# Reordering the loads of the second batch, and three edits to the chains of the first two batches, in a linear-attention and mixer kernel

## The chip, the cores and the metric

The kernel runs on one core of a Trainium2 chip. The metric is device time in microseconds (us). A ratio below is the mean time of one kernel's fast runs over the mean time of the fast runs of the kernel before in the same rounds on the same chip, so it is not quite the ratio of the medians quoted beside it (plain means of the listed runs give it within 0.001). Runs over 1.5% above the fastest of their kernel count as slow and are in no ratio. "Clock" is the mean granted TensorE clock of a run, 1 for full speed.

## The reference, cut to what matters

```python
# 8 batches, 8 heads, 576 positions, head width 64
q_p = phi(q); k_p = phi(k)            # relu times cos(pos), relu times sin(pos), side by side
kv  = einsum('bhsf,bhsd->bhfd', k_p, v)
z   = sum(k_p, axis=2)
x   = einsum('bhsf,bhfd->bhsd', q_p, kv) / (einsum('bhsf,bhf->bhs', q_p, z) + 1e-6)
u   = x + V^T U^T x                    # low-rank mixing over the positions
out = u + relu(u @ w_ch1) @ w_ch2      # w_ch1 is 512 x 2048, w_ch2 is 2048 x 512
```

The 576 positions are handled as four blocks of 128 (the "main" part) and a tail of 64. A main load of one batch is 1 MiB in 1 KB rows, a tail load 128 KB in 256 B rows.

## The kernel before: the parts concerned

TensorE runs a long stream of 512-wide matmuls: `g1` (u times w_ch1) and `g2` (hidden times w_ch2). Attention of a later batch is threaded into that stream. Only the first two batches have nothing to hide behind: `chain0` is batch 0's attention, `chain1` is batch 1's, woven into batch 0's `g1`. In the code, `V_`, `A_` and `G_` are VectorE, ScalarE and GpSimd.

```python
    V_four("X", 1)
    V_evac(V_)                                   # VectorE: V from PSUM to SBUF
    ...
    a0 = chain0()                                # GpSimd issues w1_load(0) just ahead, w1_load(1) in here
    alloc_q(1)
    load_main(qst[1], q, 1)                      # all of batch 1 on SyncE's queue
    load_tail(qt[1], q, 1)
    ...
    chain_end(0, a0)
    g1_main(0, 0, True)                          # first use of w1's first block
    ...
    def chain1(fill):
        kv_unit(1, 0, "T", 1)                    # heads 0-3: needs k features and v_ext
        fill(0)
        rec0 = den_unit(1, 0, 4, "X", 1)
        v_block(1, 4, 8, 0, 4, A_)
        ...                                      # kv_unit(1, 1) for heads 4-7 later
    ...
        at(2, lambda: v_prep(1, 0, H, (4,), (G_,)))     # GpSimd casts v's tail first ...
        at(2, lambda: v_block(1, 0, 4, 0, 4, G_))       # ... and then heads 0-3 of v's main part
```

GpSimd executes in order.

## Time and profile before

| | kernel before |
|---|---|
| time, first three runs | 319.07 us median (318.75 to 319.55) |
| span of the profile | 317.3 us |
| TensorE idle in the first 65 us / in the rest | 5.46 / 2.78 us |
| first `g1` matmul / first kv of batch 1 complete | 22.88 / 34.94 us |

The table is read from the front: TensorE is full once batch 1 is through, so a change to the front is worth what it moves the stream of `g1` matmuls, and no more. In the stretch from 22 to 36 us TensorE is busy for 11.92 of 14 us. The columns of such a line are the stretch, its length, then busy time and count of instructions of TensorE, its weight loads, VectorE, ScalarE and GpSimd, then clock, DMA share and GB/s:

```profile
22.00:36.00 14.00, 11.92 (x119) 7.11 (x119) 10.52 (x21) 11.10 (x18) 6.41 (x9) 1.00 1.18 250
```

### The profile page before, as it was taken

The numbers are of one execution on the slowest core, as the hardware profiler recorded it, in microseconds if no ns is written. First come the engines' busy times: TensorE is split into PE (matmuls) and PEld (weight loads), VectorE is DVE, ScalarE is ACT, GpSimd is POOL, SyncE is SP. The second block draws the span as 40 slices with busy tenths as digits, with TensorE's granted clock in tenths as the row PEclk, the third lists the DMA queues.
The fourth block names the chain that finished last, engine by engine and source line by source line (L and its number), as shares of the span: only waits on it lengthen the run. The fifth ranks groups of instructions, "written<-read, shape, count | busy, mean of one in ns | idle before, by whom it ended". The sixth has DMA issues, their size and how long they took to land.

```text
span 317.3 us, 5795 instructions
## 1 busy us (share of the span) xinstructions
PE 308.8 (97%) x2380; PEld 162.0 (51%) x2380; DVE 155.8 (49%) x355; ACT 151.5 (48%) x261; POOL 35.8 (11%) x67
## 2 busy tenths in 40 slices
PE   7979899999999999999999999999999999999996
PEld 3546554475545444474455444574454444464443
DVE  8769653843877554037826584254736510001211
ACT  5939655686806256659300187559300166650000
POOL 4405202100121220000121100000121100000000
PEclk9999999999999999999999999999999999999999
DMA  7999999954386928950999469900691130001122
GB/s 226 328 258 274 199 234 340 332 166 164 94 189 169 297 67 190 262 195 2 206 249 315 179 130 230 331 5 33 157 192 66 68 83 0 2 0 68 66 89 77
DMA packets 83803, 51.82 MB, mean 163 GB/s; under 512 B 52066, under 2 KB 81026, under 8 KB 83778
## 3 DMA queue, kind: packets, MB, share of 16 engines
q1 hardware_dynamic: 76850, 40.05, 46.7%
q0 software_dynamic: 6784, 11.35, 15.1%
q8 instruction: 18, 0.29, 0.4%
q10 hardware_dynamic: 144, 0.07, 0.1%
q14 instruction: 7, 0.06, 0.1%
HBM read 36.86 MB, written 9.44 MB: 146 GB/s over the span
## 4 chain that ended last, share of the span: by engine, by line
PE 87%; DMA 5%; ACT 4%; SPq 1%; DVE 1%; POOL 0%; issue 0%; DVEq 0%; ACTq 0%
PE o_ps L543 39%; PE g_ps L491 33%; PE gt_ps L511 4%; DMA w_bf<-in_moe_w_ch_dram 3%; PE kv_ps L262 3%; PE va_ps L407 3%; PE x_ps L363 3%; DMA vst<-in_v_dram 2%; ACT hid L500 2%; PE a_ps L390 1%; PE t_ps L279 1%; ACT k_p L228 1%; ACT q_p L228 1%; SPq L81 1%; SPq L75 0%; POOL mark L738 0%
## 5 line engine op out<-in xcount | busy, mean ns | idle before, releaser
L500 ACT ACTIVATE hid<-g_ps 128x512 bf16<-128x512 f32 x128 | 76.2, 596 | 100.8 <-PE g_ps L491 100.4
L491 PE MATMUL g_ps<-uT,w_bf 128*128 128x512 bf16 x512 | 118.5, 379 | 0.8 <-DMA w_bf<-in_moe_w_ch_dram 0.8
L543 PE MATMUL o_ps<-w_bf,hid 128*128 128x512 bf16 (+2 forms) x528 | 119.2, 373 | 0.0
L491 PEld LDWEIGHTS <-w_bf 128*128 128x128 bf16 x512 | 48.7, 98 | 56.8 <-DMA w_bf<-in_moe_w_ch_dram 1.0
L543 PEld LDWEIGHTS <-hid 128*128 128x128 bf16 x528 | 48.6, 98 | 52.8 <-issue 1.7
L553 DVE TENSOR_TENSOR o_sb<-u_bf,o_ps 128x512 f32<-128x512 bf16 (+2 forms) x33 | 22.1, 669 | 62.7 <-PE o_ps L543 62.7
L563 POOL DMA_DIRECT2D out_dram<-o_sb x24 | 13.4, 560 | 165.7 <-DVE o_sb L553 155.6
L408 DVE TENSOR_TENSOR u_bf<-x_bf,va_ps 128x512 bf16<-128x512 bf16 x32 | 21.8, 687 | 10.1 <-PE va_ps L407 10.1
L105 DVE CAST kv<-kv_ps 128x260 bf16<-128x260 f32 x14 | 6.0, 429 | 32.6 <-PE kv_ps L262 32.6
L373 DVE TENSOR_TENSOR x_bf<-x_ps,rec 128x512 bf16<-128x512 f32 x24 | 16.6, 691 | 0.8
L228 ACT ACTIVATE q_p<-qst,sinw 128x512 bf16<-128x512 f32 (+1 forms) x24 | 15.1, 658 | 2.2 <-DMA qst<-in_q_dram 2.1
L511 PE MATMUL gt_ps<-uT_tl,w_bf 128*128 128x128 bf16 x256 | 15.6, 219 | 0.0
L407 PE MATMUL va_ps<-A_sb,V_bf 128*128 128x512 bf16 x40 | 15.2, 379 | 0.0
L543 PE MATMUL o_ps<-w_bf,hid_tl 128*128 128x512 bf16 x64 | 15.1, 379 | 0.0
L313 DVE TENSOR_SCALAR rec<-x_ps 128x8 f32<-128x8 f32 (+1 forms) x30 | 5.0, 165 | 20.2 <-PE x_ps L363 20.1
L511 PEld LDWEIGHTS <-w_bf 128*128 128x128 bf16 x256 | 14.6, 98 | 0.5
L262 PEld LDWEIGHTS <-k_p 128*128 128x128 bf16 x256 | 11.5, 97 | 5.8 <-ACT k_p L228 1.2
L262 PE MATMUL kv_ps<-v_ext,k_p 128*128 128x65 bf16 x256 | 12.5, 193 | 1.6 <-ACT k_p L228 0.9
L230 DVE TENSOR_SCALAR k_p<-kst,cosw 128x512 bf16<-128x512 f32 (+1 forms) x31 | 14.0, 474 | 0.0
L518 ACT ACTIVATE hid_tl<-gt_ps 128x512 bf16<-128x512 f32 x16 | 9.4, 598 | 5.5 <-PE gt_ps L511 5.5
L363 PEld LDWEIGHTS <-q_pT 128*128 128x128 bf16 x192 | 9.1, 98 | 5.6 <-issue 0.6
L179 PE MATMUL w_ps<-zero 128*128 128x512 bf16 x35 | 10.7, 443 | 1.2 <-DVE U_bf L162 1.2
(106 smaller groups left out, 255.4 us busy)
## 6 DMA issues: line engine op xcount, KB each, us to landing
qst<-in_q_dram SPq DMA_DIRECT2D x7, 1024.0 KB, 8.7
kst<-in_k_dram SPq DMA_DIRECT2D x7, 1024.0 KB, 7.4
vst<-in_v_dram SPq DMA_DIRECT2D x6, 1024.0 KB, 8.3
out_dram<-o_sb POOLq DMA_DIRECT2D x24, 256.0 KB, 3.0
w_bf<-in_moe_w_ch_dram POOLq DMA_DIRECT2D x8, 512.0 KB, 9.9
vst<-in_v_dram SPq DMA_DIRECT2D x4, 512.0 KB, 7.6
out_dram<-o_sb SPq DMA_DIRECT2D x7, 256.0 KB, 2.3
qst<-in_q_dram SPq DMA_DIRECT2D x2, 512.0 KB, 3.7
```

The costliest lines, as they stand in the source:

```text
L228: nc.scalar.activation(out=o, in_=i, func=AF.Relu, bias=0.0, scale=w)
L230: eng.tensor_scalar(out=o, in0=i, scalar1=0.0, scalar2=w, op0=ALU.max, op1=ALU.mult)
L262: nc.tensor.matmul(out=acc[:, i, :], lhsT=k_p[b][:, c, h, :] if c < 4 else k_tl[:, h, :], rhs=vx[:, c, h, :], start=(c == 0), stop=(c == 4),)
L363: nc.tensor.matmul(out=acc[:, g, i * E : i * E + E], lhsT=qT_of(b, c, h), rhs=kv_sb[b][:, h, :], start=True, stop=True,)
L373: nc.vector.tensor_tensor(out=x_of(b, c, rows).rearrange("p (g i d) -> p g i d", g=2, d=D), in0=view[:, :, :, 0:D], in1=rec[rows].unsqueez ...
L407: nc.tensor.matmul(out=va, lhsT=V_bf[:, c, :], rhs=A_sb[b], start=True, stop=True)
L408: nc.vector.tensor_tensor(out=u_bf[b][:, c, :] if c < 4 else u_tl[b // 2][rows, :], in0=x_of(b, c, rows), in1=va[rows, :], op=ALU.add,)
L491: nc.tensor.matmul(out=g_ps.rearrange("p (c t) -> p c t", c=4), lhsT=w1_bf[:, d, j * P : j * P + P], rhs=uT[b][:, :, d, :], start=(d == 0) ...
L500: nc.scalar.activation(out=hid[b][:, j, :], in_=g_ps, func=AF.Relu, bias=0.0, scale=1.0)
L511: nc.tensor.matmul(out=g_ps[:, jj, :], lhsT=w1_bf[:, d, j * P : j * P + P], rhs=uT_tl[pr][:, d, :], start=(d == 0), stop=(d == 3),)
L543: nc.tensor.matmul(out=o[:, cols], lhsT=lhs[:, j, c * P : c * P + P], rhs=w2_bf[:, j, cols], start=(j == 0), stop=(j == NJ - 1),)
L553: nc.vector.tensor_tensor(out=o_sb[:, cols], in0=u[:, cols], in1=o[:, cols], op=ALU.add)
```

## The change

The intent: load what is needed first, first. Batch 1's main blocks and w1 go into one queue (GpSimd's, called the software queue, q0 in the profile) in order of use. The three tails stay on SyncE's hardware queue (q1), held back by a tiny DMA until batch 0's first reciprocals exist. Besides, V leaves PSUM behind v's cast, one x row goes to ScalarE, and batch 1's k features are made for heads 0-3 first, those of heads 4-7 behind the first kv.

```diff
     V_four("X", 1)
-    V_evac(V_)
...  in chain0
         v_block(0, 0, 4, 0, 3, V_)
+        V_evac(V_)
...
+        load_main(qst[1], q, 1, eng=G_)
         w1_load(1)
+        load_main(kst[1], k, 1, eng=G_)
+        load_main(vst[1], v, 1, 0, 4, G_)
+        load_main(vst[1], v, 1, 4, 8, G_)
+        w1_load(2)
+        nc.sync.dma_start(out=mark2, in_=rec0[0:1, 0, 0:1])
+        load_tail(qt[1], q, 1)
+        load_tail(kt[1], k, 1)
+        load_tail(vt[1], v, 1)
...
-            xh_unit(0, c, 4, 8, rec1, *(O2, O2, G3)[n])
+            xh_unit(0, c, 4, 8, rec1, *(O2, O2, G3)[n], A_ if n == 1 else None)
...  in chain1
+        for c in ORD[:3]:
+            k_prep(1, c, (V_, None), 4, 8)
         kv_unit(1, 0, "T", 1)
+        for c in ORD:
+            k_prep(1, c, (None, A_), 4, 8)
+        v_block(1, 4, 8, 0, 4, A_)
         fill(0)
         rec0 = den_unit(1, 0, 4, "X", 1)
-        v_block(1, 4, 8, 0, 4, A_)
+        for c in ORD[3:]:
+            k_prep(1, c, (V_, None), 4, 8)
...  in the main stream
-    alloc_q(1) ... all loads of batch 1 on SyncE's queue
-        at(..., lambda c=c, n=n: k_prep(1, c, (V_, A_)))
+        at(..., lambda c=c: k_prep(1, c, (V_, A_), 0, 4))
-    at(2, lambda: [w1_load(2), w1_load(3)])
+    at(6, lambda: w1_load(3))
```

More of the change, by code (lines that the diff above doesn't have):

```diff
@@ L672, in chain0 @@
         v_block(0, 4, 8, 2, 4, A_)
+        alloc_q(1)
+        alloc_k(1)
+        alloc_v(1)
+        load_main(qst[1], q, 1, eng=G_)
         w1_load(1)
+        load_main(kst[1], k, 1, eng=G_)
[6 more added lines that the diff above has]
+        load_tail(vt[1], v, 1)
         for n, c in enumerate(TL):
@@ L740 @@
     a0 = chain0()
-    alloc_q(1)
-    load_main(qst[1], q, 1)
-    load_tail(qt[1], q, 1)
-    alloc_k(1)
-    load_main(kst[1], k, 1)
-    load_tail(kt[1], k, 1)
-    alloc_v(1)
-    load_tail(vt[1], v, 1)
-    load_main(vst[1], v, 1, 0, 4)
-    load_main(vst[1], v, 1, 4, 8)
     chain_end(0, a0)
@@ L770 @@
         at(1 + n, lambda c=c, tg=tg: qtr_unit(1, c, eng=V_, tag=tg[0], bufs=tg[1]))
-        at((4, 5, 5, 6, 6)[n], lambda c=c, n=n: k_prep(1, c, (V_, A_)))
-    at(2, lambda: G_.tensor_copy(out=mark, in_=q_tlT[0:TS, 0, TS : TS + 1]))
-    at(2, lambda: [w1_load(2), w1_load(3)])
+        at((4, 5, 5, 6, 6)[n], lambda c=c: k_prep(1, c, (V_, A_), 0, 4))
     at(2, lambda: v_prep(1, 0, H, (4,), (G_,)))
     at(2, lambda: v_block(1, 0, 4, 0, 4, G_))
+    at(6, lambda: w1_load(3))
     at(6, lambda: [w2_load(n) for n in range(4)])
```

## The prediction

> **What bounds the kernel now.** I read the page first, then PE's waits, the table by stretches, the chain in order of time, the timeline of the first 50 us, and last the DMA queues in short stretches. From the page, the table by stretches, and the waits of PE in the first 130 us:
>
> ```profile
> PE 308.8 (97%) x2380; PEld 162.0 (51%) x2380; DVE 155.8 (49%) x355; ACT 151.5 (48%) x261; POOL 35.8 (11%) x67
> 0.00:65.00 65.00, 59.54 (x577) 33.36 (x578) 45.83 (x118) 43.28 (x82) 16.36 (x32) 1.00 1.09 269
> 65.00:317.00 252.00, 249.22 (x1807) 128.69 (x1804) 109.99 (x238) 108.27 (x180) 19.48 (x35) 1.00 0.50 136
> PE kv_ps L262 <- ACT k_p L228: 0.9, 2, 0.5
> PE g_ps L491 <- DMA w_bf<-in_moe_w_ch_dram: 0.8, 1, 0.8
> PE t_ps L279 <- DVE q_p L230: 0.7, 1, 0.7
> PE kv_ps L262 <- DVE v_ext L105: 0.5, 1, 0.5
> PE d_ps L321 <- ACT kv L103: 0.5, 1, 0.5
> ```
>
> TensorE is busy for 97% of the span. It is idle for 65.00 - 59.54 = 5.46 us in the first 65 us and for 2.78 us in the other 252. Everything the diff touches lies before 50 us, so its whole prize is inside those 5.46 us, of which 1.19 us pass before the first matmul. The matmuls themselves are the same in number and order in both kernels (I compared the two instruction streams of TensorE). This bounds the gain at about 4 us of 319, 1.3%.
>
> The first 65 us is also where the DMA is full: its mean share is 1.09 there against 0.50 afterwards. The waits that the change aims at, from the timeline:
>
> ```profile
> 9.61 0.82 DVE L105 CAST V_bf<-v_ps 128x640 bf16<-128x640 f32 x1 [0.69 <-PE v_ps L194]
> 12.58 0.55 DVE L105 CAST v_ext<-vst 128x768 bf16<-128x768 f32 x1
> ...
> 22.87 0.11 PEld L491 LDWEIGHTS <-w_bf 128*128 128x128 bf16 x2 [1.01 <-DMA w_bf<-in_moe_w_ch_dram]
> ...
> 33.64 0.10 PEld L262 LDWEIGHTS <-k_p 128*128 128x128 bf16 x1 [0.65 <-ACT k_p L228]
> ...
> 34.26 0.20 PE L262 MATMUL kv_ps<-v_ext,k_p 128*128 128x65 bf16 x1 [0.41 <-ACT k_p L228]
> ```
>
> A number in brackets is the idle time ahead of the row and who ended it. The first w1 block is issued by GpSimd at 13.12 and lands at 22.83: the chain of waits gives it 9.72 us. The queue table for 15 to 16, 16 to 17 and 17 to 25 us says why:
>
> ```profile
> q1 hardware_dynamic: 346, 0.35, 109.0%
> ...
> q0 software_dynamic: 6, 0.01, 3.6%
> ...
> q0 software_dynamic: 978, 0.98, 72.7%
> q1 hardware_dynamic: 1029, 0.93, 43.1%
> ```
>
> Columns are packets, MB written, share of 16 engines. Until 16.8 us only batch 1's q moves, on SyncE's queue; then w1 and batch 1's k alternate packet by packet, so each gets half the engines. The order is not the order of use.
>
> **What the Trainium skill says.** (1) "DMA: Bandwidth & Descriptors", Queues, rings and completion order: an engine round-robins between queue rows at packet granularity. The trace agrees: 978 against 1029 packets in 17 to 25 us. The same page, Issuing engines are not separate DMA queues: issuing from several engines adds no bandwidth. So one queue means order, not speed. (2) "SBUF — State Buffer", the box on the "DVE blocks DMA" trap: VectorE's two-port operations keep GpSimd from writing descriptors for its DMAs. The trace shows 3.7 us from issue to the first w1 packet, with VectorE busy for nearly all of 13.98 to 18.0, but also q1 full until 16.7; it does not say which of the two delays it. (3) "VectorE: DVE Perf Modes", The TRN2 errata: a fixed extra time per ScalarE or VectorE instruction. The trace agrees: on ScalarE a 128x512 k feature costs 0.72 us reported (about 0.61 from start to start), a 128x256 one 0.49 (about 0.43); a half costs more than half.
>
> **The change part by part.**
>
> *V evacuated later.* 0.82 us of VectorE leaves the front of v's cast. The cast starts at 12.58 now; the first v half landed at about 11.83, so it can start at 11.88, and VectorE's work ahead of it, moved up by 0.8, ends at about 11.85. It then ends at 12.43. The warm-up matmuls on TensorE end at 12.71, so the first kv starts there and not at 13.18: 0.47 us. The evacuation fits between 12.43 and 13.25, before the kv sums (13.47) want VectorE. Second v half and second k half land at 15.0 and 13.3, early enough, so the 0.47 travels on.
>
> *One x row to ScalarE.* In the second half of chain 0, VectorE loses one of five x multiplies (0.41 us) and ScalarE takes four 128x64 activations (0.93 us for the same set in the first half) where it sits idle for 0.98 us. VectorE's last x ends 0.41 + 0.47 us earlier. TensorE then goes on without the 0.2 to 0.4 us pauses around 21 us and reaches the first g1 matmul at about 21.4 instead of 22.88, if w1 is there: 1.4 us up to this point (0.84 of it the wait for w1).
>
> *Loads in one queue.* The order becomes w1(0), q, w1(1), k, v halves, w1(2), with the three tails on SyncE after the first reciprocals. Rates from the trace: q1 alone moves 0.36 MB/us; w1/w2 alone 0.205 MB/us written (3.09 MB in 30 to 46 us), so a 0.52 MB block takes 2.6 us; a 1.05 MB q or k takes 2.9; the tails (0.39 MB of small packets, 0.24 to 0.28 MB/us around 25.5 us) take 1.6 together. q1's bytes summed up to the end of v's second half of batch 0 reach that point at 13.7 us. After it, the changed kernel has only w1(0), whose first packets I put at 15.4 (2.3 us after issue; it was 3.7 and, for w1(2), 2.4). So the DMA idles for about 1.7 us where it was full. From there, with 1.3 us from last packet to landing: w1(0) 18.0, landing 19.3; q 20.9 plus the tails 22.5, landing 23.8; w1(1) landing 26.4; k 29.3; first v half 30.7; second 32.2; w1(2) 34.8.
>
> Against the needs: w1(0) at 21.4, met. q: its first main feature ran at 24.98, so -1.2 at best. w1(1) at about 26.8, met. k was used from 30.5, so -1.2. v half: GpSimd's cast of 1.04 us ends at 31.8; kv began at 32.89. w1(2): block 8 of g1 ran at 35.97 to 36.1; w1(2) at 34.8 lets it start 1.3 us earlier and no more.
>
> *k features by halves.* Ahead of kv(1,0) ScalarE has 5 half features, 5 x 0.43 = 2.2 us, instead of 3.4 (k_tl 0.72, k_p 1.33 and 1.32), and VectorE likewise. The two waits of 0.53 and 0.41 us inside kv go: 0.94 us. The later halves bring 2.2 us of ScalarE behind kv; it now idles 1.38 + 0.51 + 0.28 us between 35.65 and 39.0, so they fit without a wait for the second kv.
>
> *Sum.* 1.4 at g1's start plus 0.94 at kv would be 2.3 us, if the DMA did not matter. The landing of w1(2) caps it: all loads together are the same bytes over the same 16 engines, delivered about 1.7 us later in total because of the idle start. The cap gives 1.3 us. Behind 50 us nothing changes: TensorE is full and keeps the shift. So 319.07 - 1.3 = 317.8 us.
>
> **The rivals.** (a) *Transfers are not the limit*: w1(0) starts by 14.5 and the gain is the full 2.3 us: 316.7. For it: w1(0) began exactly when q's bulk packets ended, so the backlog of q1 may have held it, and that is gone. (b) *A new wait takes the place of the old one*: the software queue starts as late as before (16.8), or is slower with q's, k's and v's 1 KB pieces than q1 (no transfer of that kind is in this trace; w1's pieces are 1 KB written and 2 KB read, about 205 packets/us alone, against 350 on q1). Then q, v or w1(2) become the wait: first transposes of batch 1, kv(1,0) or g1's block 8, and the time is 319 to 320.5. For it: at 205 packets/us q takes 5 us instead of 2.9. Against it: the share of 118 to 125% of the engines at 205 packets/us says that those packets are just bigger jobs. (c) *ScalarE becomes the bound in chain 1* because of the later halves, two v_block and x work: a few tenths at most, since the slack above is 2.2 us; 318.2.
>
> **Range and chances.** Rival (a) sets the low end, a mix of the expected case with (b) the high end: 316.4 to 319.4. Both a gain and a loss of over 2% (6.4 us) are outside what 5.46 us of idle time, or one or two landings late by a few us, can do. Faster than 2%: 0.01; within: 0.97; slower: 0.02.
>
> **What would show each step.** V: the first kv without its 0.48 us wait for v_ext, starting at about 12.7. x and w1: first g1 matmul at 21.2 to 21.6, no wait for w_bf there. Queue: q0 from about 15.4 without a break to some 50 us, q1 nearly empty in 20 to 40; k landing at 29 to 30. Halves: no wait for k_p in kv(1,0); 128x256 ScalarE k features behind it. Cap: a wait of about 1 us for w_bf before g1's block 8, near 34.8. Wrong if TensorE waits at the transposes of q or at kv for over 1 us, if g1 starts after 22.5, or if the first 65 us have as much idle time as now.

## The result, and the profile after

The changed kernel took 323.84 us median of six runs (321.31 to 324.25), the kernel before 319.41 (318.75 to 324.39): ratio 1.0117, 95% interval 1.0069 to 1.0165. The ratio leaves out the slow run of 324.39; with it, it would be 1.009. It is slower by about 1%, where I had predicted 0.4% faster. The profiled execution ran 321.40 us with a span of 319.6 us. It is one of the two fastest of the six, so its trace accounts for 2.3 us of loss and not for the 4.4 us between the medians.

TensorE's waits in the first 130 us, to be held against those of the kernel before:

```profile
PE kv_ps L262 <- POOL v_ext L105: 2.1, 1, 2.1
PE w_ps L179 <- DVE U_bf L162: 1.2, 1, 1.2
PE t_ps L279 <- DVE q_p L230: 0.5, 1, 0.5
PE d_ps L321 <- ACT kv L103: 0.5, 1, 0.5
PE v_ps L189 <- DMA V<-in_moe_V_dram: 0.4, 1, 0.4
PE t_ps L279 <- ACT q_tl L228: 0.4, 1, 0.4
```

The two waits that the change aimed at are gone (w1 at the first `g1`, 0.8 us, and ScalarE's k features at kv, 0.9 us). In their place stands a wait of 2.1 us of kv for GpSimd. The timeline shows what GpSimd itself waited for, and what came behind it on TensorE:

```profile
21.66 0.59 PE L491 MATMUL g_ps<-uT,w_bf 128*128 128x512 bf16 x2
...
32.73 0.61 POOL L105 CAST v_ext<-vt 64x512 bf16<-64x512 f32 x1 [11.84 <-DMA vt<-in_v_dram]
33.40 1.04 POOL L105 CAST v_ext<-vst 128x1024 bf16<-128x1024 f32 x1
34.50 0.57 PE L262 MATMUL kv_ps<-v_ext,k_p 128*128 128x65 bf16 x4 [2.12 <-POOL v_ext L105]
...
36.60 1.87 PE L491 MATMUL g_ps<-uT,w_bf 128*128 128x512 bf16 x4
...
38.71 1.39 PE L491 MATMUL g_ps<-uT,w_bf 128*128 128x512 bf16 x4
```

Read it from the top. The first `g1` matmul runs at 21.66, 1.22 us earlier than before, and nothing waits for w1. Then GpSimd stands for 11.84 us on v's tail, a load of 128 KB. It was issued at 18.27 and landed 14.4 us later:

```profile
18.27 0.59 SPq L81 DMA_DIRECT2D vt<-in_v_dram  x1
```

The cast of v's main part has no wait of its own behind that: its data was there, and it stood behind the tail in GpSimd's order. By the packet records the last packet of the half of v that kv needs started at 29.3 us, the last one of v's tail at 32.2. No run changed the order of the two casts.

The queues between 22 and 32 us (packets, MB written, share of the 16 engines) show why a small load takes so long:

```profile
DMA packets 2461, 3.13 MB, mean 313 GB/s; under 512 B 1249, under 2 KB 1946, under 8 KB 2459
## 3 DMA queue, kind: packets, MB, share of 16 engines
q0 software_dynamic: 1275, 2.82, 94.3%
q1 hardware_dynamic: 1184, 0.29, 17.7%
```

Packets again alternate, 1275 against 1184. But SyncE's packets are rows of 256 B, one each, and the software queue's are 1 KB (w1) or 4 KB (q, k and v: four rows together). An equal share of turns gave SyncE's queue 0.29 of 3.13 MB. A tail has 64 x 8 = 512 rows, so 512 / 16 engines = 32 turns. The median duration of a packet in the records is 18 ns for 256 B, 98 ns for w1's and 159 ns for 4 KB. That makes, as an estimate, 32 x (98 + 18) = 3.7 us beside w1 and 32 x (159 + 18) = 5.7 us beside k and v; the records, counted off in order, have k's tail from 22.5 to 26.4 (3.9 us, mostly beside w1) and v's tail from 26.4 to 32.2 (5.8 us). The engines do not keep step, so a tail lands later than this count says: k's at 28.8. No run changed the size of the packets, so this price of a turn is read from the records and not shown by an experiment.

There is a second cost behind the wait. The four `g1` matmuls at 36.60 take 1.87 us and not 1.03. The clock column, the third from the end, says why; the first fence is the kernel before, the second the changed one:

```profile
30.00:40.00 10.00, 8.76 (x123) 5.44 (x120) 6.85 (x15) 7.19 (x13) 3.89 (x5) 1.00 1.22 204
```

```profile
30.00:40.00 10.00, 7.57 (x74) 3.93 (x72) 5.45 (x16) 6.84 (x14) 5.33 (x7) 0.83 0.85 147
```

The mean clock in this stretch is 0.83: the records have 3.4 us at half clock, from 36.0 to 39.4. Against the kernel before, the stream is 0.61 us late when the first kv of batch 1 is done (its kv sums start to be read at 35.59, before at 34.98), and 2.05 us late at the end of chain 1 (the first `g1` matmuls behind its last transposes: 52.92 against 50.87). Nearly all of the difference arises in one place: from the first matmul that uses the sums to the second kv it is 4.11 us (36.07 to 40.18), before 2.75 (35.46 to 38.21). So in this trace about 0.6 us of the loss is the wait net of what was gained, and 1.4 us is the half clock.

### The profile page after: what moved, and what is told of

It is laid out like the page before. It is cut to its first block, busy times and chain, and to the rows that moved or that the text cites. A ratio compares the mean times of both kernels' runs of the same rounds, so it can differ in the third digit from the quotient of the medians.

```text
span 319.6 us, 5812 instructions
## 1 busy us (share of the span) xinstructions
PE 310.3 (97%) x2380; PEld 162.4 (51%) x2380; DVE 155.3 (49%) x359; ACT 153.6 (48%) x270; POOL 38.2 (12%) x70
## 4 chain that ended last, share of the span: by engine, by line
PE 86%; issue 4%; DMA 2%; POOL 2%; ACT 2%; SPq 1%; DVE 1%; POOLq 0%; DVEq 0%
PE o_ps L543 39%; PE g_ps L491 31%; PE gt_ps L511 4%; PE kv_ps L262 3%; PE va_ps L407 3%; PE x_ps L363 3%; DMA vst<-in_v_dram 2%; PE a_ps L390 1%; ACT hid L500 1%; SPq L81 1%; ACT q_p L228 1%; POOL v_ext L105 1%; PE t_ps L279 1%; POOL w_bf L91 0%; POOL vst L75 0%
## 5 line engine op out<-in xcount | busy, mean ns | idle before, releaser
L491 PE MATMUL g_ps<-uT,w_bf 128*128 128x512 bf16 x512 | 119.7, 382 | 0.0
L228 ACT ACTIVATE k_p<-kst,sinw 128x256 bf16<-128x256 f32 (+1 forms) x23 | 11.9, 570 | 0.4 <-DMA kst<-in_k_dram 0.3
```

The source lines that it names most:

```text
L228: nc.scalar.activation(out=o, in_=i, func=AF.Relu, bias=0.0, scale=w)
L491: nc.tensor.matmul(out=g_ps.rearrange("p (c t) -> p c t", c=4), lhsT=w1_bf[:, d, j * P : j * P + P], rhs=uT[b][:, :, d, :], start=(d == 0) ...
```

## The experiments

All ratios are to the kernel before in the same rounds. "Low clock" counts the runs with a mean clock below 0.997, the slow ones included.

| run | chip | median us | ratio, 95% interval | low clock |
|---|---|---|---|---|
| the change, first measured | | 323.84 | 1.0117, 1.0069 to 1.0165 | 6 of 6 |
| after_again | 14 | 322.50 | 1.0066, 1.0020 to 1.0112 | 5 of 6 |
| after_c | 4 | 323.02 | 1.0070, 1.0027 to 1.0114 | 5 of 6 |
| queue_only | 14 | 323.33 | 1.0096, 1.0061 to 1.0131 | 5 of 6 |
| mark_v | 14 | 321.51 | 1.0060, 1.0024 to 1.0096 | 6 of 6 |
| pad_rows | 15 | 323.64 | 1.0130, 1.0096 to 1.0165 | 6 of 6 |
| warm12 | 10 | 322.26 | 1.0031, 0.9986 to 1.0076 | 1 of 6 |
| warm12_b | 4 | 321.66 | 1.0044, 0.9990 to 1.0098 | 2 of 6 |
| front_only | 10 | 320.85 | 0.9987, 0.9942 to 1.0032 | 4 of 6 |
| halves_only | 14 | 319.06 | 0.9968, 0.9931 to 1.0005 | 0 of 6 |
| front_halves | 15 | 318.65 | 0.9966, 0.9929 to 1.0002 | 0 of 6 |
| cold_front | 15 | 318.79 | 0.9973, 0.9943 to 1.0004 | 6 of 6 |
| vt_sw | 4 | 319.88 | 0.9974, 0.9928 to 1.0021 | 1 of 6 |
| tails_sw | 10 | 319.44 | 0.9931, 0.9889 to 0.9973 | 0 of 6 |
| tails_sw_b | 4 | 319.51 | 0.9972, 0.9916 to 1.0028 | 3 of 6 |
| no_mark | 10 | 319.03 | 0.9906, 0.9854 to 0.9958 | 1 of 6 |
| no_mark_b | 15 | 318.63 | 0.9975, 0.9938 to 1.0012 | 2 of 6 |

The kernel before had a low clock in 8 of 11, 3 of 11, 4 of 11 and 4 of 11 runs on chips 10, 14, 15 and 4. Its median on chip 10 was 321.31 us, on the others 319.91, 320.09 and 320.75. A ratio from chip 10 flatters a kernel that keeps its clock, so I compare such kernels on more than one chip.

### Are the tails starved?

*tails_sw*: the three tails go into the software queue too, each ahead of its main block.

```diff
+        load_tail(qt[1], q, 1, eng=G_)
         load_main(qst[1], q, 1, eng=G_)
         w1_load(1)
+        load_tail(kt[1], k, 1, eng=G_)
         load_main(kst[1], k, 1, eng=G_)
+        load_tail(vt[1], v, 1, eng=G_)
         load_main(vst[1], v, 1, 0, 4, G_)
...
-        load_tail(qt[1], q, 1)
-        load_tail(kt[1], k, 1)
-        load_tail(vt[1], v, 1)
```

> Changed kernel with the three 64-row tails of batch 1 moved from SyncE's queue into the software queue, each just ahead of its main block. Theory (tails starve: their 256 B packets get one turn per 1 to 4 KB packet of the software queue, so v's tail lands at 32.7 us and GpSimd, which casts it first, holds the first kv of batch 1 until 34.5): the wait of kv for GpSimd's v_ext goes or is under 0.5 us, kv starts at about 32, no lowered clock between 36 and 40, and the time is 3 to 4 us under the changed kernel, about 0.995 of the kernel before. Rival (the software queue as such is too slow or too late, q, k and v main blocks would come just as late): kv still starts after 34 us and the time stays at 1.007 to 1.015 of the kernel before.

Measured: 0.9931, no low clock in six runs. GpSimd's two casts and TensorE's waits:

```profile
30.67 0.62 POOL L105 CAST v_ext<-vt 64x512 bf16<-64x512 f32 x1 [7.60 <-DMA vt<-in_v_dram]
31.74 1.04 POOL L105 CAST v_ext<-vst 128x1024 bf16<-128x1024 f32 x1 [0.46 <-DMA vst<-in_v_dram]
```

```profile
PE kv_ps L262 <- POOL v_ext L105: 1.0, 2, 0.9
...
PE g_ps L491 <- DMA w_bf<-in_moe_w_ch_dram: 0.4, 1, 0.4
```

Now v's main part is the later of the two (0.46 us behind the tail), as it should be; kv waits 0.9 us, more than the 0.5 us I expected, but starts at 32.84 and not at 34.50:

```profile
32.84 0.54 PE L262 MATMUL kv_ps<-v_ext,k_p 128*128 128x65 bf16 x4 [0.88 <-POOL v_ext L105]
```

The software queue sends the same 256 B rows packed: the packet records have 32 packets of 4 KB more per tail, where SyncE's queue sent 512 packets. The rival, that the software queue is simply too late, falls. The small wait for w1 at 35.40 is the cap of my prediction, here in its place and with 0.4 us.

*tails_sw_b*, the same kernel on chip 4:

> All three tails in the software queue. Theory: ratio 0.992 to 0.998, under v's tail alone by the wait for q's tail. Rival: no better than v's tail alone.

Measured: 0.9972 (0.9916 to 1.0028), against 1.0070 for the changed kernel in the same batch. Three of its six runs had a low clock, which the first measurement did not show. It did not come out clearly below *vt_sw* (0.9974), so that part of the expectation is not confirmed.

*vt_sw*: v's tail alone goes into the software queue.

```diff
+        load_tail(vt[1], v, 1, eng=G_)
         load_main(vst[1], v, 1, 0, 4, G_)
...
-        load_tail(vt[1], v, 1)
```

> Changed kernel with v's tail alone moved into the software queue, ahead of v's main block; q's and k's tails stay on SyncE. Theory (v's tail is what holds kv): its wait for v_ext falls to under 1.2 us and no wait for k's tail takes its place (k's tail ends near 26.5 us); what is left is the wait for q's tail (0.4 to 2.7 us in the traces so far); ratio 0.994 to 1.001. Rival (kv then waits for k's tail or v's main block as long): ratio within 0.003 of the changed kernel's.

Measured: 0.9974, against 1.0070 for *after_c* on the same chip. The wait for GpSimd is gone, and what is left is the expected wait for q's tail, and 0.6 us for ScalarE's k:

```profile
PE t_ps L279 <- ACT q_tl L228: 1.6, 1, 1.6
...
PE kv_ps L262 <- ACT k_p L228: 0.6, 1, 0.6
```

The second of these was not expected. I had k's tail through near 26.5 us; its last 32 packets started between 27.8 and 30.7, and ScalarE waited for it:

```profile
31.36 0.50 ACT L228 ACTIVATE k_tl<-kt,sinw 64x256 bf16<-64x256 f32 x1 [0.55 <-DMA kt<-in_k_dram]
```

So on SyncE's queue k's tail is late as well.

*no_mark*: the tails stay on SyncE but are not held back, so they leave before the software queue is busy.

```diff
-        nc.sync.dma_start(out=mark2, in_=rec0[0:1, 0, 0:1])
         load_tail(qt[1], q, 1)
```

> Changed kernel without the small DMA that holds back the tails until the first reciprocals, so that SyncE sends q's and k's tail right behind batch 0's loads, before the software queue is busy. Theory (tails starve only because they meet the software queue's large packets): tails of q and k land before 18 us, v's before 27, the wait of kv for v_ext goes, and the time is 0.993 to 0.997 of the kernel before. Rival (GpSimd's cast waits for something else, or v's main block is the late one): kv still begins after 33.5 us, ratio above 1.003.

Measured: 0.9906, better than expected, on the chip that flatters. q's and k's tail packets ran from 13.3 to 17.3 us and v's from 17.3 to 19.3; GpSimd cast v's tail at 21.73 without waiting:

```profile
21.73 0.62 POOL L105 CAST v_ext<-vt 64x512 bf16<-64x512 f32 x1
32.01 1.05 POOL L105 CAST v_ext<-vst 128x1024 bf16<-128x1024 f32 x1 [9.67 <-DMA vst<-in_v_dram]
```

The first kv of batch 1 had no wait. A new one of 1.3 us appeared at the second kv of batch 0, for GpSimd's cast of batch 0's second v half, which waited for its data until 16.28 (15.04 in the kernel before): the early tails ride in the same queue and their packets began before that load's last ones.

*no_mark_b*, the same on chip 15:

> The best version so far once more on this chip, beside the halves alone. Theory: 0.988 to 0.994, lower than the kernel with the old loads, because g1 starts earlier when w1's first block need not share the engines. Rival (the order of loads is worth nothing once the tails are not starved): the same ratio as the front edits and halves with the old loads, within 0.002.

Measured: 0.9975, and *front_halves*, with the old loads, 0.9966 on the same chip. The rival holds: no gain of the new order of loads is seen once the tails are not starved. The two intervals are 0.4% to either side, and no_mark_b has a wait of its own (1.2 us at the second kv of batch 0), so a gain of a few tenths of a per cent is not excluded.

*mark_v*: SyncE holds the tails until the second v half of batch 0 has landed, a middle way.

```diff
-        nc.sync.dma_start(out=mark2, in_=rec0[0:1, 0, 0:1])
+        nc.sync.dma_start(out=mark2, in_=vst[0][0:1, H - 1, 0, 0:1])   # ahead of the allocations
```

> Changed kernel in which SyncE holds the tails back until the second v half of batch 0 has landed (about 15 us) and not until the first reciprocals. Theory: the tails start about 17 us, take one turn per packet of the software queue (some 3.7 us each), so q's lands near 21, k's near 25, v's near 29, ahead of v's main block; no wait of kv for v_ext above 0.5 us, nothing of the 1.3 us wait of the second kv of batch 0 that the version without the holding DMA had; ratio 0.987 to 0.994. Rival (only a start before the software queue helps): v's tail still lands after 31 us and kv waits over 1 us, ratio above 1.0.

Measured: 1.0060; my expectation was wrong and the rival right. The tails' first packet ran at 18.9, q's tail ended at 21.9, k's at 25.4, v's at 32.2; kv waited 2.4 us. I had given each tail 3.7 us; the last one, beside 4 KB packets, took 6.8. They were issued only 0.6 us earlier than in the changed kernel (16.16 against 16.77) and started 2 us earlier, which did not help v's tail: it still ran beside k's and v's main blocks.

*pad_rows*: 16 unused elements behind each head in the landing tiles, meant to keep the software queue's packets at 1 KB.

```diff
-        vst[b] = pool.tile([P, H, 4, D], FP32, tag="vst", bufs=1, name="vst")
+        vst[b] = pool.tile([P, H, 4 * D + 16], FP32, tag="vst", ...)[:, :, 0 : 4 * D].rearrange(...)
# kst and qst likewise
```

> Changed kernel with 16 unused elements behind each head's 256 in the landing tiles of q, k and v, so that the software queue's packets of these blocks can be no longer than 1 KB; the order of all loads stays. Theory (a tail of 512 packets needs 32 turns on each engine, and each turn waits for one packet of the software queue: 159 ns for 4 KB, 46 to 98 ns for 1 KB): v's tail takes 2 to 4 us instead of 5.8 to 6.8 and is through by 28 to 30.5 us instead of 32.2 to 33.9; the wait of kv for v_ext falls under 1 us; ratio 0.994 to 1.002. Rival (the tails are late because they start late or rank behind the software queue, whatever its packets): v's tail ends after 31.5 us, ratio above 1.004.

Measured: 1.0130, v's tail cast at 34.04. This run tells nothing about the theory: the edit did not do what it was for. The records still have 768 packets of 4 KB in the software queue, as in the changed kernel; gaps in the landing tile do not stop it from packing four rows into a packet.

### Which part of the change does what?

*after_again* and *after_c* are the changed kernel once more.

> The changed kernel once more, beside the others of this batch. Theory: v's tail lands at 32 to 34 us, kv of batch 1 waits 1.5 to 2.5 us for GpSimd's v_ext, the mean granted clock is 0.989 to 0.995 (one or two stretches of about 3.4 us at half clock), ratio 1.003 to 1.013. Rival (the loss of the first measurement was chance): ratio below 1.001.

> The changed kernel on this chip, as the measure for the other three: ratio 1.004 to 1.013, mean clock 0.989 to 0.995 in most runs.

Measured: 1.0066 and 1.0070, so the loss is not chance. The place of the wait moves. In the profile of after_again kv waits 0.5 us for v_ext, less than expected, and TensorE stands 2.0 us for q's tail. In the profile of after_c, TensorE stands at the transposes for q's tail, not at kv; k's and v's tails follow in the same queue and are late too, but the stall before has already cost the time:

```profile
PE t_ps L279 <- ACT q_tl L228: 3.3, 1, 3.3
```

*queue_only*: the loads of the changed kernel, everything else as before.

```diff
# from the changed kernel: V_evac back ahead of the k features, the x row back on VectorE,
# k_prep(1, c, (V_, A_)) for all heads, v_block(1, 4, 8, ...) behind den_unit
```

> The changed kernel with V's evacuation, the x row and the halves of k undone: only the loads differ from the kernel before. Theory (the loss is all in the order of the loads): kv of batch 1 still waits over 1 us for v_ext, ratio 1.004 to 1.014, at or above the changed kernel's. Rival (the halves of k or the moved V take part in the loss): ratio at least 0.004 below the changed kernel's of this batch.

Measured: 1.0096, not below the changed kernel's 1.0066; its profile has both waits, 2.7 us for q's tail and 2.0 us for v_ext. The loss is all in the loads. So is the earlier start of `g1`: here it comes at 21.44, without either front edit, in the changed kernel at 21.66.

```profile
21.44 0.59 PE L491 MATMUL g_ps<-uT,w_bf 128*128 128x512 bf16 x2
```

*halves_only*: the kernel before with k's halves alone.

```diff
+        for c in ORD[:3]:
+            k_prep(1, c, (V_, None), 4, 8)
         kv_unit(1, 0, "T", 1)
+        for c in ORD:
+            k_prep(1, c, (None, A_), 4, 8)
+        v_block(1, 4, 8, 0, 4, A_)
...
+        for c in ORD[3:]:
+            k_prep(1, c, (V_, None), 4, 8)
```

> Kernel before with only k's features by halves. Theory: both waits of kv for ScalarE's k features (0.9 us in the profile before) go, the later halves cost nothing, and the ratio is 0.996 to 0.999. Rival (the later halves on ScalarE and VectorE delay block 8 of g1 or the second kv by as much as the first gains): ratio 1.000 or more, with a new wait for ScalarE before 42 us.

Measured: 0.9968. Against the eight runs of the kernel before at full clock alone it is 0.6 us less (means of 318.83 and 319.44). The wait of kv for ScalarE's features fell from 0.9 to 0.2 us, and ScalarE's later halves ran in a row without anyone waiting for them; the row of four 128x256 features of 1.71 us is the later half of the main part:

```profile
32.81 0.89 ACT L228 ACTIVATE k_p<-kst,sinw 128x256 bf16<-128x256 f32 x2
33.61 0.57 ACT L500 ACTIVATE hid<-g_ps 128x512 bf16<-128x512 f32 x1
34.20 0.50 ACT L228 ACTIVATE k_tl<-kt,sinw 64x256 bf16<-64x256 f32 x1
34.71 1.71 ACT L228 ACTIVATE k_p<-kst,sinw 128x256 bf16<-128x256 f32 x4
```

*front_only*: V's evacuation and the x row alone.

```diff
-    V_evac(V_)
...
         v_block(0, 0, 4, 0, 3, V_)
+        V_evac(V_)
...
+            xh_unit(0, c, 4, 8, rec1, *(O2, O2, G3)[n], A_ if n == 1 else None)
```

> Kernel before with only the chain of batch 0 changed: V evacuated behind v's cast and the second x row on ScalarE. Theory: the first kv and the x rows come up to 0.5 us earlier, but the first g1 matmul still waits for w1's first block, which lands at 22.8 as before, so the ratio is 0.998 to 1.001. Rival (the two front edits alone are worth what I predicted, some 0.5 us or more): ratio below 0.998.

Measured: 0.9987 (0.9942 to 1.0032), no difference. The wait for w1's first block is 1.2 us in its profile against 0.8 before:

```profile
PE g_ps L491 <- DMA w_bf<-in_moe_w_ch_dram: 1.2, 1, 1.2
```

That is no gain given back, since TensorE was ready for `g1` no earlier: this wait began at 22.4 us, before at 22.0. In this run v's first half landed later (cast at 13.05 after a wait for it, before at 12.58). And the x row saves VectorE nothing: from the second denominators to the tail's x multiply it takes 2.15 us with the edit (18.95 to 21.10) and without it (18.61 to 20.76). In place of the multiply stands a wait for TensorE's products, in the changed kernel too (18.39 to 20.54):

```profile
20.20 0.42 DVE L349 TENSOR_TENSOR x_bf<-xh_ps,rec 128x256 bf16<-128x256 f32 x1 [0.46 <-PE xh_ps L338]
```

*front_halves*: both, with the old loads.

> Kernel before with the two front edits and k's halves, but the old loads. Theory: halves alone gave 0.9968, the front edits are hidden behind w1's first block: ratio 0.994 to 0.999, and a wait of over 0.5 us for w1 before the first g1 matmul. Rival (the parts add up and the new order of loads is not needed for them): ratio below 0.993.

Measured: 0.9966, the same as the halves alone, with waits of 1.4 us for w1 in two places. The front edits add nothing.

### Is the half clock a cost of the idle stretch?

*warm12*: 12 dummy matmuls and not 2 ahead of batch 1's first kv.

```diff
-    at(7, lambda: keep_warm(2, "X", 1))
+    at(7, lambda: keep_warm(12, "X", 1))
```

> Changed kernel with 12 instead of 2 warm-up matmuls ahead of batch 1's first kv, which fill TensorE's idle 2.1 us but take no wait away. Theory (the lowered clock between 36 and 40 us, which doubles the time of some g1 matmuls, follows from that idle stretch, and is worth 1.4 us): kv still starts at about 34.5, the granted clock stays 1.00, and the time is 1.2 to 1.6 us under the changed kernel, 1.002 to 1.005 of the kernel before. Rival (the clock drop has nothing to do with the idle stretch, or the whole loss is the wait): the time is the changed kernel's or longer.

Measured: 1.0031. The profiled run had its clock at 1.00 throughout, and five of six runs 0.998 or more. kv did not start at 34.5 but at 35.94, because both tails landed later in that run. In that trace the stream is 1.41 us behind the changed kernel's at the reading of kv (37.48 against 36.07) and 0.10 us behind at the second kv (40.28 against 40.18): the 1.3 us between are the half clock that did not come.

*warm12_b*, beside after_c on chip 4:

> 12 warm-up matmuls ahead of kv of batch 1. Theory (half clock is a second cost of the same idle stretch): mean clock 0.998 or more in most runs, and 0.002 to 0.005 under the changed kernel's ratio. Rival (the stretch at half clock costs nothing, because TensorE then waits for others anyway, as in the version without the front warm-up): the same ratio as the changed kernel within 0.002 at the higher clock.

Measured: 1.0044 (0.9990 to 1.0098) against 1.0070 (1.0027 to 1.0114) at the higher clock in four of six runs. The direction is that of the theory, but the intervals overlap, so the share of the half clock in the loss is not settled by times alone. It rests on the traces.

The clock of all runs tells one thing more. Of the 43 fast runs of the kernel before on the four chips, 18 had a low clock and took 321.7 us on the mean, the 25 others 319.6. The changed kernel had a low clock in 15 of its 17 fast runs. So a good part of its loss is that it is nearly always in a state in which the kernel before is in under half of its runs. Idle stretch and half clock come together, so these means do not part the two costs. No run of the kernel before with a low clock was profiled: what brings it there stays open.

*cold_front*: halves_only, which never had a low clock, without the 14 dummy matmuls at 9.7 us. No work waits for them.

```diff
     q_prep(0, 4, (V_, A_))
-    keep_warm(14, "o", 2)
```

> The version with k's halves alone, which showed a granted clock of 0.999 or more in all six runs, without the 14 warm-up matmuls at 9.7 us; nothing waits for them. Theory (an idle stretch of TensorE of 2 us or more brings a stretch of about 3.4 us at half clock): TensorE idles 3 to 4 us before the first kv, the clock is 0.5 for about 3.4 us beginning within 2.5 us of its end, the mean is 0.993 to 0.996 in most runs. The time rises by less than 1.7 us, since TensorE waits for others there: ratio 0.997 to 1.002. Rival (the half clock comes at random or from something else): mean clock 0.999 or more in most runs, ratio as the halves alone, about 0.997.

Measured: all six runs have a low clock, where halves_only had none. The stretch from 8 to 20 us, first halves_only, then cold_front:

```profile
8.00:20.00 12.00, 9.92 (x159) 6.53 (x158) 8.96 (x27) 8.97 (x21) 3.04 (x5) 1.00 1.16 294
```

```profile
8.00:20.00 12.00, 6.94 (x107) 5.39 (x105) 8.12 (x24) 8.54 (x20) 3.17 (x5) 0.72 1.06 274
```

```profile
14.22 0.38 PE L262 MATMUL kv_ps<-v_ext,k_p 128*128 128x65 bf16 x4 [4.18 <-DVE v_ext L105]
```

TensorE idles 4.18 us and gets 6.8 us at half clock, from 11.6 to 18.4. An idle stretch does bring the half clock. The stretch came out twice as long as I expected and began inside the idle time, not after it. The time was not longer (0.9973): in that stretch TensorE waits for others anyway. Half clock costs time where TensorE is the one that others wait for, as between 36 and 39 us of the changed kernel.

Over all traces: five have an idle stretch of TensorE between 2.0 and 3.0 us at kv or at the transposes (the changed kernel, after_again, mark_v, pad_rows, and queue_only with two), and each has a stretch of 3.4 or 6.8 us at half clock that begins within 2.1 us of the end of such an idle stretch or just before it. In queue_only the first of its two was not followed by one. after_c and cold_front, with longer idle stretches (3.35 and 4.18 us), have 6.8 us each, which begin inside the idle time. In the traces whose longest wait is under 1.7 us there is none before the end of the kernel. By the clock records, each stretch starts a whole number of steps of 3.41 us after the first record of its trace (in the changed kernel nine, from 5.32 to 36.04) and lasts one or two steps; so it can begin after the idle time or inside it. In six of the seven traces TensorE was idle for 2.0 to 2.5 us of the step before. In queue_only it was 1.7, and an earlier step there with 2.0 was not followed, so the exact condition is not shown.

## Why the prediction was wrong, point by point

- **What bounds the kernel.** Right: the whole effect lies before 50 us. But I took the 5.46 us of idle time as a bound for the gain and wrote of losses only as "landings late by a few us"; that idle time itself lowers the clock was not among the terms. Two of my own signs of being wrong came: a wait of over 1 us at kv (2.1), and as much idle time in the first 65 us as before (5.93 us, before 5.46).
- **V evacuated later.** Right as a mechanism, uncertain in size. It presumes that the first v half lands at 11.83. In the changed kernel's profile VectorE waited 0.49 us for that half until 12.61, and kv started at 13.22, as late as before. In no_mark, where it landed by 11.98, kv started at 12.71, the predicted time.
- **x row and start of `g1`.** The number is near (21.66 us, predicted 21.2 to 21.6) and the wait for w1 is gone as predicted, but the rest is luck. Of the 1.22 us, 1.0 is that wait; the other 0.22 is a wait for VectorE's k features at the second kv of batch 0 that was not in my sum. Neither front edit shows in this trace: the first kv was as late as before, and the x row, predicted to save VectorE 0.41 us, saved nothing. queue_only, without both, starts `g1` at 21.44.
- **Start of the software queue.** I said 15.4; it was 14.67, 1.5 us after issue, right at the end of SyncE's backlog. Nothing in that trace points to VectorE as the cause of the old 3.7 us.
- **The step that failed** is the term "the tails (0.39 MB of small packets, ...) take 1.6 together", and with it the sign of the kernel "q1 nearly empty in 20 to 40". I priced the tails by bytes at the rate of a queue that is alone. They are paid in turns: 512 packets, 32 turns per engine, each behind a packet of 1 or 4 KB. They started about where I had put them (21.1, predicted 20.9), but together they took until 32.2 us, 11.1 and not 1.6. The skill's round robin "at packet granularity" stood in my own text; I used it for equal packets and did not apply it to unequal ones. I even wrote that each queue gets half the engines, over lines that show 72.7% against 43.1% for nearly equal numbers of packets. v's tail was missing from my list of landings against needs, and it is GpSimd's first cast: kv, which was to gain 0.94 us, waited 2.1 us for it.
- **Landings of the main blocks.** Right within about a microsecond: counted off in order, the last packets of k, of v's first half and of w1(2) started at 27.9, 29.3 and 34.1 us, predicted 28.0, 29.4 and 33.5. The cap by w1(2) is real (0.4 us in tails_sw) but was hidden behind the larger wait.
- **k by halves.** Right: predicted 0.94 us, halves_only gave 0.32% of 320 us, 1.0 us, with an interval that just touches 1; against full-clock runs alone it is 0.6.
- **Rivals.** (a) had the start of w1's first block nearly right (by 14.5, measured 14.67), but not the gain. (b) named the right kind of outcome, a new wait in place of the old, and 319 to 320.5 us, but for the wrong reason: it looked for slow main blocks in the software queue. My reason against it (bigger jobs per packet) was exactly what harmed the tails. (c) did not happen.
- **The range.** Its high end, 319.4, is below even some runs of the kernel before, of which fast ones reach 320.34 in the first measurement. I took three runs within 0.8 us as the spread.

## What to carry to other kernels

Before moving a large transfer to another queue, look at the small ones that stay behind: where queues take turns by packet, a load of many short rows paid here about one packet of the other queue for each of its rows, so put it into the same queue ahead of its consumer, or have it through before the large packets start. List every landing that an in-order engine waits for, the small ones too, since one late 128 KB load holds everything behind it. And in a kernel whose matmul engine is full, an idle stretch of two microseconds can cost again afterwards at half clock, so check the clock column beside the waits.

## What the Trainium skill lacked or had wrong

- "DMA: Bandwidth & Descriptors", Queues, rings and completion order, has the round robin at packet granularity, and the runs agree (1275 against 1184 packets in 22 to 32 us). It lacks the consequence: the same turns were 2.82 and 0.29 MB, and a 128 KB load took 14.4 us to land.
- The same page, SWDGE vs HWDGE vs iDMA, gives packets of "≤4096 B preferably" for the software path. The runs agree: the rows of q, k and v, of 256 B and of 1 KB, went out as 4 KB packets there (w1's, written as 1 KB rows, as 1 KB packets). It lacks that the hardware queue sent each 256 B row as a packet of its own (512 for a tail, against 32).
- The same page, Latency and other measured facts, gives first bytes after about 0.6 us on the hardware path and 1 us on the software path. With the other queue full, the first packet came 3.7 us after issue for w1 in the kernel before, and 4.3 us for q's tail in the changed kernel (issued at 16.77, first packet at 21.1); what held the tail back that long, no run shows.
- "TensorE: Matmul & The Clock Gate", Part 1, says that the clock falls after at least one idle window of about 3.4 us. The lengths agree (3.4 and 6.8 us at half clock), the condition does not: idle stretches of 2.0 to 2.4 us were followed by it in four traces. Why one of 2.75 us in queue_only was not, stays open.
